# Attention in steps of two groups: the order of the matmuls, the maxima and the copies on each engine

## The chip, the core and the metric

The kernel is one program on one core of a Trainium2 chip. The metric is the time of one execution on the device, in microseconds (us). The core has five engines that each work through their own list of instructions in order and meet only through semaphores: TensorE (PE; its weight loads are shown apart as PEld), VectorE (DVE), ScalarE (ACT), GpSimd (POOL) and SyncE (SP), which here only issues DMAs. Matmul results land in PSUM, which has eight banks; each result tile here takes one bank.

## The reference: what is computed

Attention over 4 batches, 12 heads, 448 positions and head size 64, in which the heads are mixed before and after the softmax, and behind it two feed-forward parts without a softmax (1792 tokens, 768 wide):

```python
scores = scale * np.matmul(q, k.transpose(0, 1, 3, 2))
scores = np.einsum('bhij,hg->bgij', scores, w_pre)
scores = scores - np.max(scores, axis=-1, keepdims=True)
attn = np.exp(scores)
attn = attn / (np.sum(attn, axis=-1, keepdims=True) + 1e-09)
attn = np.einsum('bhij,hg->bgij', attn, w_post)
x = np.matmul(attn, v)          # then, after a transpose to (tokens, 768):
h = (x @ w1) * (x @ w2) @ w3 @ w_out
g = np.maximum(0.01 * (h @ w_in), h @ w_in)
out = g @ w_out2
```

## The kernel before

The queries of a batch are dealt into chunks of 120, 120, 120 and 88. A chunk is cut into **blocks** of ten queries and pairs of blocks form a **group** of twenty queries; there are 180 blocks in 92 groups (six groups a chunk, five in the short one, whose last group has one block). These kinds of work make up the attention:

- `qk`: the scores of a pair of heads for a whole chunk, two chunks ahead (tile `pq`, L221, two banks `qa`); ScalarE copies them out (`evict`, L229), and they are stored to DRAM (`sdr`).
- `relayout` (L262): a group's scores come back from DRAM with queries times heads on the partitions (tile `sr`), four groups ahead.
- `premix` (L273): the first mixing of heads as a matmul with `kpre`; a block's result fills one bank `pm`.
- `softmax`: VectorE takes the maximum of each row (`mx`, L280), ScalarE the exponential with its sum (`e`, `sm`, L283). `weigh`: GpSimd adds 1e-9 to the sum (L290), VectorE takes the reciprocal `rc` (L292), GpSimd multiplies it into the mixing weights (`kr`, L294).
- `postmix` (L308): the second mixing, four matmuls a block in the program (the trace has two records for each matmul of this kind), result in a bank `po`; VectorE or ScalarE copies it to `ap` (L315).
- `av` (L328): the product with `v` for two heads; two of them share a bank `px`, which VectorE copies to `y` (L337). It needs the whole chunk's `ap`.
- `conversions` (the generator `filler`): the weights for the later parts are turned from 64-bit words to 32-bit on ScalarE and VectorE (tile `wc`, L98 to L109) in small steps between the other work; `q_split` and `k_split` split inputs in two parts (VectorE L80, L185).

The attention is under a manual schedule, so each engine's instructions stand in the order of the code. The main loop takes one group a step: the maxima and exponentials of group k, then the `postmix` of group k-2 block by block between the `weigh` calls of group k, then one `qk`, in every other step two `av`, and `premix` of group k+1. Copies out of `po` go to VectorE, but for the second block of every other step. `px` has a bank of its own.

At the end the loop runs out of `qk`, and the first weights of the next part, `fold` (L542), are prepared: `wo` in eight pieces (L553, L554) and `ws` from `wc`. `marks` and `ends` hold instructions of the loop behind which these are placed.

Of the kernel before, what the change touches and what calls it, by code (L numbers as in the profile page):

```python
# [23 lines left out]
def attention_moe_kernel(ctx: ExitStack, tc, qt, kt, vt, w_pre, w_post, w1, w2, w3t, w_out, w_in2, w_out2, out):  # L24
# [7 lines left out]
    nc = tc.nc  # L32
# [11 lines left out]
    AHEAD, QAHEAD, START, LAG = 4, 2, 7, 2  # L44
# [26 lines left out]
    banks = {"qa": 2, "pm": 3, "po": 2, "px": 1}  # L71
# [50 lines left out]
    def attention():  # L122
        with ExitStack() as es:
# [50 lines left out]
            srt, pms, ets, sms, krs, apt = {}, {}, {}, {}, {}, {}  # L174
# [101 lines left out]

            def softmax(n):
                pm = pms.pop(n)
                mx = wk.tile([P, 1], F32, tag="mx", name="mx")
                nc.vector.tensor_reduce(out=mx, in_=pm, axis=AX.X, op=ALU.max, negate=True)  # L280
                e = wk.tile([P, S], F32, tag="e", name="e", bufs=6)
                sm = wk.tile([P, 1], F32, tag="sm", name="sm")
# [5 lines left out]
            def weigh(n):  # L288
                sm = sms.pop(n)
                nc.gpsimd.tensor_scalar(out=sm, in0=sm, scalar1=1e-9, scalar2=None, op0=ALU.add)  # L290
                rc = wk.tile([P, 1], F32, tag="rc", name="rc")
# [7 lines left out]
            def postmix(n, copy):  # L299
# [15 lines left out]
                copy(ap[:, :, :, o:o + nb], po)  # L315

            def av(b, c, p):
# [5 lines left out]
                if r == 0:  # L323
                    pxs[0] = bank("qa" if g and (b, c) == order[-1] else "px", [P, 2, CH], "px")
# [115 lines left out]
            q_split(0, 2)()  # L440
            premix(0)
            todo, since = [], 0
            for k in range(NG + LAG):
# [3 lines left out]
                evict()  # L447
                if k < NG:
                    b, c, t, nt = where[k]
                    ci = order.index((b, c))  # L450
                    for n in groups[k]:
                        softmax(n)
                done = k - LAG
                for i in range(2):
                    if done >= 0 and i < len(groups[done]):
                        on_act = i and (t % 2 or k >= NG - 8)
                        postmix(groups[done][i], nc.scalar.copy if on_act else nc.vector.tensor_copy)
                    if k < NG and i < len(groups[k]):
                        weigh(groups[k][i])
                if k < NG:  # L460
                    if k + AHEAD < NG:
                        relayout(k + AHEAD)
                    ps = []
                    if ci + QAHEAD < len(order):
                        ps = [t] if nt == NPAIR else [4, 5] if t == 4 else [t]
                        if ci == 0:
                            ps = ([], [0], [1], [2], [3], [4, 5])[t]
                    if ps:
                        qk(*order[ci + QAHEAD], ps[0])
                since += 1  # L470
                if ci + QAHEAD < len(order):
                    n = 2 * (since % 2)
                else:
                    n = 1 if k < NG and len(todo) <= nt - since + 1 else 2
                for _ in range(min(n, len(todo))):
                    av(*todo.pop(0))
                if done >= 0 and done < NG - 1 and where[done][2] == where[done][3] - 1:
                    todo += [(*where[done][:2], p) for p in range(NPAIR)]
                    since = 0
                if k < NG:  # L480
                    for p in ps[1:]:
                        qk(*order[ci + QAHEAD], p)
                    if k + 1 < NG:
                        premix(k + 1)
# [10 lines left out]
                if k < NG:  # L495
                    if c == 0 and t == 2:
                        v_prep(b)
# [266 lines left out]
```

## Time and profile before

| | |
|---|---|
| median of 3 runs | 1332.93 us (1329.87 to 1333.66) |
| the profiled execution | 1328.94 us, of which its span of instructions is 1327.2 us |
| TensorE busy | 1309.5 us, 99% of the span |
| VectorE, ScalarE, GpSimd busy | 882.1, 599.7 and 168.1 us |
| mean granted TensorE clock | 0.992 of full speed |
| DMA | 220.01 MB, mean 166 GB/s |

A view of the timeline has one line for instructions of one kind that follow each other: start, time from the first start to the last end, engine, line of the kernel, operation, tiles written and read, shape, number, and in brackets how long the engine had been idle and what ended that. Matmuls overlap in the array: one that takes 0.27 us can start 0.10 us behind the one before, so the pace is read from starts, not from durations.

### The profile page before, as it was taken

Reading aid. Unit: us, or ns where it says so; the run is one execution under the profiler, and the core shown is the slowest. Engines: PE = TensorE matmul, PEld = TensorE weight load, DVE = VectorE, ACT = ScalarE, POOL = GpSimd, SP = SyncE. Lnnn points to the kernel's source line nnn. Section 1 sums busy time; section 2 is a strip of 40 time slices with the busy share of each in tenths; the row PEclk is TensorE's granted clock in tenths of the full one; section 3 lists DMA queues with packets and bytes.
Section 4 is the critical chain, followed back from the end, with each engine's and each line's share of the span. In section 5 each row is a group of like instructions: output and inputs, shape, how many; then the busy total and the mean of one; then the engine's idle time right before and its main releaser. Section 6 shows DMA issues by size and latency. Waiting matters only on the chain.

```text
span 1327.2 us, 23071 instructions
## 1 busy us (share of the span) xinstructions
PE 1309.5 (99%) x8926; PEld 1126.1 (85%) x8926; DVE 882.1 (66%) x1536; ACT 599.7 (45%) x1161; POOL 168.1 (13%) x371
## 2 busy tenths in 40 slices
PE   8999999999999899999999999999999999999998
PEld 5677777777777899898989999999898989999998
DVE  5577777776657676673469678695773449596762
ACT  5566666666556343332245525162433226444240
POOL 1343444444344000000000000000000000000000
PEclk8899999999999999999999999999999999999999
DMA  7988999998987763421424333256331324342302
GB/s 242 308 282 252 287 308 279 314 298 269 270 225 206 249 200 123 119 80 57 126 72 146 117 119 97 94 149 209 99 108 48 103 95 124 115 143 90 125 1 84
DMA packets 137825, 220.01 MB, mean 166 GB/s; under 512 B 20148, under 2 KB 119220, under 8 KB 137140
## 3 DMA queue, kind: packets, MB, share of 16 engines
q1 hardware_dynamic: 137716, 218.54, 53.0%
q8 instruction: 71, 1.16, 0.4%
q14 instruction: 38, 0.31, 0.1%
HBM read 161.62 MB, written 56.89 MB: 165 GB/s over the span
## 4 chain that ended last, share of the span: by engine, by line
PE 94%; DMA 3%; DVE 1%; issue 0%; SPq 0%; ACT 0%; POOL 0%; ACTq 0%; POOLq 0%; DVEq 0%
PE pm L630 44%; PE po L699 18%; PE po L308 11%; PE pm L273 6%; PE px L328 5%; PE pq L221 5%; PE pw L565 5%; DMA sr<-sdr 1%; DMA ws<-w3s 1%; DMA ql<-in_q_dram 1%; PE turn L254 1%; DMA sdr<-s 0%; SPq L262 0%; ACT e L283 0%; DVE wc L106 0%
## 5 line engine op out<-in xcount | busy, mean ns | idle before, releaser
L630 PE MATMUL pm<-x,ws 128*128 128x512 f32 (+1 forms) x2304 | 466.8, 363 | 0.0
L630 PEld LDWEIGHTS pm<-x,ws 128*128 128x128 f32 x2304 | 417.6, 188 | 47.7
L699 PE MATMUL po<-ws,g 128*128 128x384 f32 x1344 | 234.2, 334 | 0.0
L699 PEld LDWEIGHTS po<-ws,g 128*128 128x128 f32 x1344 | 233.1, 188 | 0.0
L308 PEld LDWEIGHTS po<-kr,e 128*112 128x112 f32 x1440 | 155.9, 179 | 67.3 <-POOL kr L294 26.1
L308 PE MATMUL po<-kr,e 128*112 128x120 f32 (+1 forms) x1440 | 173.4, 274 | 1.8 <-DVE ap L315 1.8
L283 ACT ACTIVATE e<-pm,mx 128x448 f32<-128x448 f32 x180 | 112.7, 631 | 131.7 <-DVE mx L280 130.7
L80 DVE TENSOR_TENSOR ws<-wc,ws 128x768 fp32r<-128x768 f32 (+1 forms) x103 | 100.1, 974 | 83.7 <-ACT ws L77 83.4
L98 ACT ACTIVATE wc<-wr 128x768 f32<-128x768 f32 (+3 forms) x122 | 104.9, 863 | 80.7 <-DVE ws L80 62.7
L77 ACT ACTIVATE ws<-wc 128x768 fp32r<-128x768 f32 (+1 forms) x103 | 87.9, 857 | 106.8 <-PE po L699 74.0
L294 POOL TENSOR_SCALAR kr<-kpost,rc 128x120 f32<-128x120 f32 x180 | 125.0, 694 | 67.5 <-DVE rc L292 59.2
L280 DVE TENSOR_REDUCE mx<-pm 128x1 f32<-128x448 f32 x180 | 104.1, 617 | 22.9 <-PE pm L273 17.9
L630 PE MATMUL pm<-h,ws 128*128 128x512 f32 (+1 forms) x576 | 116.3, 363 | 0.0
L630 PEld LDWEIGHTS pm<-h,ws 128*128 128x128 f32 x576 | 104.3, 188 | 11.7
L109 DVE SCALAR_TENSOR_TENSOR wc<-wr,wc 128x768 uint32<-128x768 uint32 (+3 forms) x122 | 110.7, 908 | 1.5
L106 DVE SCALAR_TENSOR_TENSOR wc<-wr,wc 128x768 uint32<-128x768 uint32 (+3 forms) x122 | 110.2, 906 | 1.1
L273 PE MATMUL pm<-sr,kpre 60*64 60x448 f32 x720 | 96.3, 575 | 5.0 <-DMA sr<-sdr 4.9
L229 ACT ACTIVATE s<-pq 120x448 f32<-120x448 f32 (+1 forms) x180 | 88.5, 543 | 20.9 <-PE pq L221 19.8
L100 DVE TENSOR_SCALAR wc<-wc 128x768 f32<-128x768 f32 (+3 forms) x122 | 65.1, 534 | 46.2 <-ACT wc L98 46.0
L315 DVE COPY ap<-po 112x480 f32<-112x480 f32 (+1 forms) x135 | 86.8, 643 | 1.7 <-PE po L308 1.5
L328 PEld LDWEIGHTS px<-ap,vs 112*64 112x64 f32 x1536 | 75.2, 138 | 14.8 <-issue 13.2
L221 PE MATMUL pq<-ks,qs 64*120 64x448 f32 (+1 forms) x576 | 85.2, 402 | 2.2 <-ACT qs L77 1.3
(56 smaller groups left out, 980.0 us busy)
## 6 DMA issues: line engine op xcount, KB each, us to landing
sr<-sdr SPq DMA_DIRECT2D x176, 210.0 KB
sdr<-s SPq DMA_DIRECT2D x36, 840.0 KB
wr<-in_moe_w_dram SPq DMA_DIRECT2D x32, 768.0 KB
wr<-in_moe_w_in_dram SPq DMA_DIRECT2D x32, 768.0 KB
wr<-in_moe_w_out_dram SPq DMA_DIRECT2D x32, 768.0 KB
sdr<-s SPq DMA_DIRECT2D x12, 616.0 KB
wr<-in_moe_w_dram SPq DMA_DIRECT2D x7, 1024.0 KB
wr<-in_moe_w_out_dram SPq DMA_DIRECT2D x16, 384.0 KB
```

The source lines that it names most:

```text
L98: nc.scalar.activation(out=cf, in_=hi.bitcast(F32), func=ACTF.Abs)
L106: lambda: nc.vector.scalar_tensor_tensor(out=c, in0=hi, scalar=0xC0000000, in1=c, op0=ALU.bitwise_and, op1=ALU.bitwise_or),
L109: lambda: nc.vector.scalar_tensor_tensor(out=c, in0=lo, scalar=29, in1=c, op0=ALU.logical_shift_right, op1=ALU.bitwise_or),
L221: nc.tensor.matmul(pq[e][:m], qst[b, c][rows, p, x, :m], kst[b, p][rows, y, :], start=(j == 0), stop=(j == 2))
L273: nc.tensor.matmul(pms[n][g * Q:(g + 1) * Q], kpre[rows], sr[rows, g, :], start=True, stop=True)
L280: nc.vector.tensor_reduce(out=mx, in_=pm, axis=AX.X, op=ALU.max, negate=True)
L283: ends["act"] = nc.scalar.activation(out=e, in_=pm, func=ACTF.Exp, bias=mx, scale=1.0, accum_out=sm)
L294: ends["pool"] = nc.gpsimd.tensor_scalar(out=kr, in0=kpost, scalar1=rc, scalar2=None, op0=ALU.mult)
L308: nc.tensor.matmul(po[:, jc].rearrange("p h (g i) -> p h g i", g=2), e[:, jc * JP:(jc + 1) * JP], kr, start=True, stop=True,)
L328: nc.tensor.matmul(px[e * D:(e + 1) * D, r, :ni], vst[b][:, jc, 2 * p + e, :], ap[:, jc, 2 * p + e, :ni], start=(jc == 0), stop=(jc == NJ ...
L630: nc.tensor.matmul(dst, wt[:, a, kk, :], x[:, kk, c, c0:c0 + w], start=(kk == 0 and j == 0), stop=(kk == kn - 1 and j == 2),)
L699: nc.tensor.matmul(po, g[:, m, a, t * P:(t + 1) * P], wts[m][:, c, 0, cs], start=(m == 0 and j == 0), stop=(m == FQ - 1 and j == 2),)
```

## The change

The loop takes two groups, four blocks, a step. `premix` of both groups stands together at a step's end, `postmix` of the four blocks of the step before stands together, and one to three `qk` stand around them. `top` takes the four maxima, first in the step on VectorE; the exponentials stay in `softmax`. Of four copies out of `po` VectorE has the first and the third, ScalarE the second and the fourth. `px` loses its bank to `pm` (now four) and takes turns with the four blocks in the two banks `po`. What was done once a group at a step's end is moved into `side`; the conversions start with group 10, not 7, their first loads with group 5, not 2, and the loads of `v` and `k` are one group later. The pieces of `wo` are tied to other marks, and `ends` now also holds the copies.

The diff, cut (`pairs` returns the `qk` of a group as before):

```diff
-    AHEAD, QAHEAD, START, LAG = 4, 2, 7, 2
+    AHEAD, QAHEAD, START = 4, 2, 10
...
-    banks = {"qa": 2, "pm": 3, "po": 2, "px": 1}
+    banks = {"qa": 2, "pm": 4, "po": 2}
...
-                t = bank("px", [P, P], "turn")
+                t = bank("po", [P, P], "turn")
...
+            def top(n):
+                mxs[n] = wk.tile([P, 1], F32, tag="mx", name="mx", bufs=8)
+                nc.vector.tensor_reduce(out=mxs[n], in_=pms[n], axis=AX.X, op=ALU.max, negate=True)
+
             def softmax(n):
-                pm = pms.pop(n)
-                mx = wk.tile([P, 1], F32, tag="mx", name="mx")
-                nc.vector.tensor_reduce(out=mx, in_=pm, axis=AX.X, op=ALU.max, negate=True)
+                pm, mx = pms.pop(n), mxs.pop(n)
...
+                sm = wk.tile([P, 1], F32, tag="sm", name="sm", bufs=8)
...
-                copy(ap[:, :, :, o:o + nb], po)
+                ends["act" if copy == nc.scalar.copy else "dve"] = copy(ap[:, :, :, o:o + nb], po)
...
-                    pxs[0] = bank("qa" if g and (b, c) == order[-1] else "px", [P, 2, CH], "px")
+                    pxs[0] = bank("qa" if g and (b, c) == order[-1] else "po", [P, 2, CH], "px")
...
+            def side(k):
+
...
+                while lows:
+                    lows.pop(0)()
+                if c == 0 and t == (2 if b else 3):
+                    v_prep(b)
+                if (t == 4 or k == 0) and ci + QAHEAD + (1 if k == 0 else 2) < len(order):
+                    q_load(*order[ci + QAHEAD + (1 if k == 0 else 2)])
+                if b + 1 < B and c == NC - 3 and t in (2, 4, 5):
+                    k_load(b + 1, (2, 4, 5).index(t))
+                if k >= START or k == START - 5:
+                    for _ in range(2 if k >= START and t in (2, 5) else 1):
+                        next(filler, None)
+
...
             premix(0)
-            todo, since = [], 0
-            for k in range(NG + LAG):
+            premix(1)
+            todo = []
+            for k in range(0, NG + 2, 2):
+                evict()
                 flush()
                 while later:
                     stores.append(later.pop(0))
-                evict()
-                if k < NG:
-                    b, c, t, nt = where[k]
-                    ci = order.index((b, c))
-                    for n in groups[k]:
-                        softmax(n)
-                done = k - LAG
-                for i in range(2):
-                    if done >= 0 and i < len(groups[done]):
-                        on_act = i and (t % 2 or k >= NG - 8)
-                        postmix(groups[done][i], nc.scalar.copy if on_act else nc.vector.tensor_copy)
-                    if k < NG and i < len(groups[k]):
-                        weigh(groups[k][i])
-                if k < NG:
-                    if k + AHEAD < NG:
-                        relayout(k + AHEAD)
-                    ps = []
...
-                    if ps:
-                        qk(*order[ci + QAHEAD], ps[0])
-                since += 1
-                if ci + QAHEAD < len(order):
-                    n = 2 * (since % 2)
-                else:
-                    n = 1 if k < NG and len(todo) <= nt - since + 1 else 2
-                for _ in range(min(n, len(todo))):
+                now = [g for g in (k, k + 1) if g < NG]
+                done = [g for g in (k - 2, k - 1) if g >= 0]
+                ps = [x for g in now for x in pairs(g)]
+                fresh = [n for g in now for n in groups[g]]
+                old = [n for g in done for n in groups[g]]
+                if ps:
+                    qk(*ps.pop(0))
+                for g in now:
+                    if g + AHEAD < NG:
+                        relayout(g + AHEAD)
+                for n in fresh:
+                    top(n)
+                for i in (0, 2):
+                    if i == 0:
+                        for n in fresh[:2]:
+                            softmax(n)
+                        evict()
+                    elif not now:
+                        while todo:
+                            av(*todo.pop(0))
+                    for j in (i, i + 1):
+                        if j < len(old):
+                            postmix(old[j], nc.scalar.copy if j % 2 else nc.vector.tensor_copy)
+                    if i == 0:
+                        for n in fresh[2:]:
+                            softmax(n)
+                    for n in fresh[i:i + 2]:
+                        weigh(n)
+                if len(ps) > 1:
+                    qk(*ps.pop(0))
+                for g in done:
+                    b, c, t, nt = where[g]
+                    if t == nt - 1 and (b, c) != order[-1]:
+                        todo += [(b, c, p) for p in range(NPAIR)]
+                for _ in range(min(4 if len(todo) > NPAIR else 2, len(todo))):
                     av(*todo.pop(0))
-                if done >= 0 and done < NG - 1 and where[done][2] == where[done][3] - 1:
-                    todo += [(*where[done][:2], p) for p in range(NPAIR)]
-                    since = 0
-                if k < NG:
-                    for p in ps[1:]:
-                        qk(*order[ci + QAHEAD], p)
-                    if k + 1 < NG:
-                        premix(k + 1)
-                    if ci + QAHEAD + 1 < len(order) and t == (4 if ci == 0 or c == NC - 2 else 3):
-                        lows.append(q_split(*order[ci + QAHEAD + 1]))
-                    if b + 1 < B:
-                        if c == NC - 3 and t >= 4:
-                            lows.append(k_split(b + 1, t - 4))
-                        if c == NC - 2 and t < 4:
-                            lows.append(k_split(b + 1, t + 2))
+                for x in ps:
+                    qk(*x)
+                for g in (k + 2, k + 3):
+                    if g < NG:
+                        premix(g)
+                for g in now:
+                    side(g)
                 while lows:
                     lows.pop(0)()
                 marks.append(dict(ends))
...
-            tags = itertools.cycle(("pm", "qa", "po", "pm", "px", "qa", "po", "pm"))
+            tags = itertools.cycle(("pm", "qa", "pm", "po", "pm", "qa", "pm", "po"))
...
                 for kk in range(KF):
-                    with behind(ends if kk >= KF - 2 else marks[kk - LAG - KF]):
+                    with behind(marks[min(kk // 2 - 4, -1)]):
                         hi_act(wo[:, kk, 0], wo[:, kk, 1].bitcast(F32))
                         lo_dve(wo[:, kk, 1], wo[:, kk, 1].bitcast(F32), wo[:, kk, 0])
```

TensorE in the middle of the attention (`pm` is `premix`, `po` `postmix`, `px` `av`, `pq` `qk`), first before, two steps and the start of a third:

```order
L273 MATMUL pm<-sr,kpre 64x448 x4
L308 MATMUL po<-kr,e 112x120 x8
L221 MATMUL pq<-ks,qs 120x448 x6
L328 MATMUL px<-ap,vs 64x88 x16
L273 MATMUL pm<-sr,kpre 64x448 x4
L308 MATMUL po<-kr,e 112x120 x8
L221 MATMUL pq<-ks,qs 120x448 x6
```

Each group's `pm` and `po` form stretches of their own there. Of the change, one step of two groups:

```order
L273 MATMUL pm<-sr,kpre 64x448 x8
L221 MATMUL pq<-ks,qs 120x448 x6
L310 MATMUL po<-kr,e 112x120 x16
L330 MATMUL px<-ap,vs 64x120 x16
L221 MATMUL pq<-ks,qs 120x448 x6
```

The same matmuls stand in five stretches in place of seven. Over the attention the listings have 46 stretches of `pm` (91 before), 47 of `po` (92) and 45 of `px` (50).

VectorE in the middle of the attention, before, two steps (`mx` the maxima, `ap` a copy out of `po`, `rc` the reciprocals, `y` the copy out of `px`, `wc` conversions, `ks` a split):

```order
L280 TENSOR_REDUCE mx<-pm 128x1 x2
L315 COPY ap<-po 112x48x10
L292 RECIPROCAL rc<-sm 128x1
L315 COPY ap<-po 112x48x10
L292 RECIPROCAL rc<-sm 128x1
L337 COPY y<-px 128x240
L185 TENSOR_TENSOR ks<-kl,ks 128x448
L100 TENSOR_SCALAR wc<-wc 128x384
L280 TENSOR_REDUCE mx<-pm 128x1 x2
L315 COPY ap<-po 112x48x10
L292 RECIPROCAL rc<-sm 128x1 x2
```

A copy stands directly behind two maxima there. Of the change, one step and the first row of the next:

```order
L279 TENSOR_REDUCE mx<-pm 128x1 x4
L317 COPY ap<-po 112x48x10
L294 RECIPROCAL rc<-sm 128x1 x2
L317 COPY ap<-po 112x48x10
L294 RECIPROCAL rc<-sm 128x1 x2
L339 COPY y<-px 128x240
L106 SCALAR_TENSOR_TENSOR wc<-wr,wc 128x384
L109 SCALAR_TENSOR_TENSOR wc<-wr,wc 128x384
L279 TENSOR_REDUCE mx<-pm 128x1 x4
```

The first copy moved behind four maxima, the second of VectorE's copies behind two reciprocals.

VectorE at the end of the attention, from the last maximum on, before (`wo` and `wc` are weights of the next part):

```order
L280 TENSOR_REDUCE mx<-pm 128x1
L315 COPY ap<-po 112x48x10
L292 RECIPROCAL rc<-sm 128x1
L80 TENSOR_TENSOR wo<-wo 128x768
L337 COPY y<-px 128x240
L80 TENSOR_TENSOR wo<-wo 128x768
L315 COPY ap<-po 112x48x10
L100 TENSOR_SCALAR wc<-wc 128x1024 x2
L103 TENSOR_SCALAR wc<-wc 128x1024 x2
L106 SCALAR_TENSOR_TENSOR wc<-wr,wc 128x1024 x2
L337 COPY y<-px 128x240
L109 SCALAR_TENSOR_TENSOR wc<-wr,wc 128x1024
```

The last copies stand there among the pieces of `wo` and behind steps on `wc`. Of the change:

```order
L317 COPY ap<-po 112x48x10
L317 COPY ap<-po 112x48x8
L339 COPY y<-px 128x240
L80 TENSOR_TENSOR wo<-wo 128x768 x2
L100 TENSOR_SCALAR wc<-wc 128x1024 x2
L103 TENSOR_SCALAR wc<-wc 128x1024 x2
L106 SCALAR_TENSOR_TENSOR wc<-wr,wc 128x1024 x2
L109 SCALAR_TENSOR_TENSOR wc<-wr,wc 128x1024 x2
L80 TENSOR_TENSOR ws<-wc,ws 128x1024 x2
```

All copies of the attention now stand ahead of the last two `wo` and of the eight steps on `wc`.

## Rows read from the trace of the kernel before

**Rows 1.** The page, busy time and share of the span of each engine.

```profile
PE 1309.5 (99%) x8926; PEld 1126.1 (85%) x8926; DVE 882.1 (66%) x1536; ACT 599.7 (45%) x1161; POOL 168.1 (13%) x371
```

**Rows 2.** Windows: length, busy PE PEld DVE ACT POOL, granted clock, DMA share, GB/s.

```profile
200.00:300.00 100.00, 100.00 (x1059) 71.54 (x1061) 73.88 (x175) 64.83 (x166) 41.83 (x89) 1.00 0.94 300
300.00:411.00 111.00, 111.00 (x1189) 79.53 (x1181) 72.22 (x170) 66.09 (x169) 45.40 (x104) 1.00 0.89 254
411.00:447.00 36.00, 30.28 (x326) 24.82 (x327) 27.17 (x45) 17.67 (x33) 7.46 (x16) 0.95 0.68 209
```

**Rows 3.** Timeline of TensorE, some of the stretches of 203 to 222 us.

```profile
206.35 0.87 PE L221 MATMUL pq<-ks,qs 64*120 64x448 f32 x6
207.16 0.98 PE L273 MATMUL pm<-sr,kpre 60*64 60x448 f32 x8
...
212.49 0.98 PE L273 MATMUL pm<-sr,kpre 60*64 60x448 f32 x8
```

**Rows 4.** The same view in windows of a fraction of a microsecond.

```profile
203.62 0.61 PE L273 MATMUL pm<-sr,kpre 60*64 60x448 f32 x4
...
204.04 0.56 PE L273 MATMUL pm<-sr,kpre 60*64 60x448 f32 x4
204.53 0.36 PE L308 MATMUL po<-kr,e 128*112 128x120 f32 x1
...
204.72 0.57 PE L308 MATMUL po<-kr,e 128*112 128x120 f32 x4
...
205.13 0.57 PE L308 MATMUL po<-kr,e 128*112 128x120 f32 x4
```

**Rows 5.** Chain that ended last, 370 to 400 us: start, time, what.

```profile
378.00 1.79 PE px L328 x32
...
386.04 0.97 PE px L328 x16
```

**Rows 6.** Timeline of one group on four engines, 379 to 384 us.

```profile
379.72 0.98 PE L273 MATMUL pm<-sr,kpre 60*64 60x448 f32 x8
...
380.81 1.16 DVE L280 TENSOR_REDUCE mx<-pm 128x1 f32<-128x448 f32 x2 [0.56 <-PE pm L273]
...
381.88 0.65 DVE L315 COPY ap<-po 112x480 f32<-112x480 f32 x1
...
382.34 0.22 POOL L290 TENSOR_SCALAR sm<-sm 128x1 f32<-128x1 f32 x1 [2.87 <-ACT e L283]
...
382.60 0.16 DVE L292 RECIPROCAL rc<-sm 128x1 f32<-128x1 f32 x1
...
382.93 0.59 POOL L294 TENSOR_SCALAR kr<-kpost,rc 128x120 f32<-128x120 f32 x1 [0.36 <-DVE rc L292]
...
383.60 0.22 POOL L290 TENSOR_SCALAR sm<-sm 128x1 f32<-128x1 f32 x1
383.85 0.16 DVE L292 RECIPROCAL rc<-sm 128x1 f32<-128x1 f32 x1 [1.09 <-POOL sm L290]
```

**Rows 7.** Timeline where TensorE and a copy wait for each other.

```profile
427.97 0.65 DVE L315 COPY ap<-po 112x480 f32<-112x480 f32 x1
...
428.76 1.04 PE L308 MATMUL po<-kr,e 128*112 128x120 f32 x8 [1.77 <-DVE ap L315]
...
429.85 0.57 ACT L315 COPY ap<-po 112x480 f32<-112x480 f32 x1 [0.84 <-PE po L308]
```

**Rows 8.** Groups of VectorE, 66.9 to 411 us: busy us, mean ns, idle before.

```profile
L185 DVE TENSOR_TENSOR ks<-kl,ks 128x448 fp32r<-128x448 f32 x18 | 11.1, 616 | 0.0
...
L109 DVE SCALAR_TENSOR_TENSOR wc<-wr,wc 128x384 uint32<-128x384 uint32 (+1 forms) x19 | 10.6, 556 | 0.3
```

**Rows 9.** Timeline of TensorE near the start of the attention.

```profile
54.66 2.42 PE L273 MATMUL pm<-sr,kpre 60*64 60x448 f32 x8 [2.33 <-DMA sr<-sdr]
```

**Rows 10.** Windows behind it, columns as in rows 2.

```profile
57.08:62.00 4.92, 4.92 (x27) 4.02 (x30) 1.60 (x5) 2.70 (x7) 1.62 (x4) 0.58 0.99 331
```

**Rows 11.** Groups of VectorE at the end of the attention, 426 to 437 us.

```profile
L106 DVE SCALAR_TENSOR_TENSOR wc<-wr,wc 128x1024 uint32<-128x1024 uint32 x2 | 2.4, 1216 | 0.0
```

More of the change, by code (lines that the diff above doesn't have):

```diff
@@ L173, in attention @@
             kst, vst, qst, st = {}, {}, {}, {}
-            srt, pms, ets, sms, krs, apt = {}, {}, {}, {}, {}, {}
+            srt, pms, mxs, ets, sms, krs, apt = {}, {}, {}, {}, {}, {}, {}
             def k_load(b, g):
@@ L290, in weigh @@
                 nc.gpsimd.tensor_scalar(out=sm, in0=sm, scalar1=1e-9, scalar2=None, op0=ALU.add)
-                rc = wk.tile([P, 1], F32, tag="rc", name="rc")
+                rc = wk.tile([P, 1], F32, tag="rc", name="rc", bufs=8)
                 ends["dve"] = nc.vector.reciprocal(out=rc, in_=sm)
@@ L440, in attention, with pairs @@
             q_split(0, 2)()
+            def side(k):
+                b, c, t, nt = where[k]
+                ci = order.index((b, c))
+                if ci + QAHEAD + 1 < len(order) and t == (4 if ci == 0 or c == NC - 2 else 3):
+                    lows.append(q_split(*order[ci + QAHEAD + 1]))
+                if b + 1 < B:
+                    if c == NC - 3 and t >= 4:
+                        lows.append(k_split(b + 1, t - 4))
+                    if c == NC - 2 and t < 4:
+                        lows.append(k_split(b + 1, t + 2))
+                while lows:
[9 more added lines that the diff above has]
+                        next(filler, None)
+            def pairs(k):
+                b, c, t, nt = where[k]
+                ci = order.index((b, c))
+                if ci + QAHEAD >= len(order):
+                    return []
+                ps = [t] if nt == NPAIR else [4, 5] if t == 4 else [t]
+                if ci == 0:
+                    ps = ([], [0], [1], [2], [3], [4, 5])[t]
+                return [(*order[ci + QAHEAD], p) for p in ps]
             premix(0)
-            todo, since = [], 0
-            for k in range(NG + LAG):
+            premix(1)
+            todo = []
+            for k in range(0, NG + 2, 2):
+                evict()
                 flush()
@@ L494, in attention @@
                 marks.append(dict(ends))
-                if k < NG:
-                    if c == 0 and t == 2:
-                        v_prep(b)
-                    if (t == 4 or k == 0) and ci + QAHEAD + (1 if k == 0 else 2) < len(order):
-                        q_load(*order[ci + QAHEAD + (1 if k == 0 else 2)])
-                    if b + 1 < B and c == NC - 3 and t in (0, 1, 3):
-                        k_load(b + 1, (0, 1, 3).index(t))
-                    if k >= START or k == START - 5:
-                        for _ in range(2 if k >= START and t in (2, 5) else 1):
-                            next(filler, None)
             for _ in filler:
```

5 lines of the change are left out of this document (removed).

## The prediction

> **What bounds the kernel now.** I read the page first: TensorE is busy 99% of the span, no other engine over 66% [rows 1]. Then the windows of the attention: from 200 to 411 us TensorE is busy all the time at a granted clock of 1.00, VectorE 74% and 65%, ScalarE less, the DMA share .94 and .89; only the end, 411 to 447 us, has idle time, 5.7 us [rows 2]. So in the middle no wait is left to take away: time can come only out of TensorE's own work, and a new wait there costs its full length. Behind 447 us the change only permutes bank tags, and I cost that at nothing. One pair of groups takes 8.87 us (212.49 less 203.62) [rows 3, 4].
>
> **What the change saves.** The matmuls stay, but they stand in fewer stretches, and a stretch loses something at its ends. For `po` the matmuls run at .1025 us each (sets of four start at 204.72 and 205.13), so 16 should take 1.64; from 204.53 to 206.35 they take 1.82. Joining two stretches saves .18 [rows 3, 4]. For `px` 32 take 1.79 and 16 take .97, so joining saves .15 [rows 5]. A `pm` stretch takes .91, .42 for its first round and .49 for its last [rows 3, 4]; a middle round isn't shown alone, so I take .17, between the other two. A step of two groups therefore saves .35, and .50 where it joins `px` too, as at the end of the attention, where no `qk` is left.
>
> By the order 45 junctions of `pm`, 45 of `po` and 5 of `px` go: 7.7 + 8.1 + .7 = 16.5 us, 1.2%, if nothing new waits.
>
> **What the change adds: banks.** Five users now share two banks in each step: the four blocks, then `px`. Block 3 needs the bank of copy 1, `px` that of copy 3. I work a step out from durations of before; time 0 is its first `pm` matmul. `pm` 2 x .91 - .17 and `pq` .81 (206.35 to 207.16) put the first `po` matmul at S = 2.46 [rows 3, 4].
>
> Block one is ready for its copy 1.09 behind S (428.76 to 429.85); a copy on VectorE takes .65, and TensorE goes on .14 behind its end (427.97 + .65 to 428.76) [rows 7]. So the bank is back 1.88 behind S, where TensorE wants it after 2 x .91 - .09 = 1.73: it stops .15. ScalarE's copy takes .57 [rows 7], and block four comes in time.
>
> Copy three can't start before two reciprocals, which stand ahead of it in VectorE's list. The second waits for GpSimd, which handles one block after the other. By one group's timeline: copy start to reciprocal .72 (381.88 to 382.60), to `kr` .33, to the next `sm` .67, to its reciprocal .25, then about half of that one's .16 [rows 6]: copy three starts 2.05 behind copy one, and `px` 2.05 + .65 + .14 = 2.84 behind it, at S + 3.93. Unhindered it would start at S + 3.46 (two joined stretches). Each step with `qk` loses .47 and gains .35: +.12. If the reciprocals were not in the way, copy three would be ready at S + 1.88 + 1.09, `px` at S + 3.76, and the loss is .30: a net gain of .05. Both ends stay for the range.
>
> At the end there is no `pq`, S is 1.65, and the four maxima decide: the first comes 1.09 behind the first `pm` matmul (379.72 to 380.81), two take 1.07 to the copy [rows 6], so copy one starts at 3.23, not 2.74, and `px` at 6.07 against 5.11. Loss .96, gain .50: +.46.
>
> There are some 35 steps of the first kind from 62 us on and 5 of the second: 35 x .12 = +4.2 and 5 x .46 = +2.3.
>
> **Chunk ends.** In seven steps `px` reads the copy that ScalarE makes of block four. That block starts at S + 2.75, so its copy ends at S + 2.75 + 1.09 + .57 = S + 4.41 and `px` starts about .53 later than above: 7 x .53 = +3.7 (none if the first `px` of a chunk can go a step later; it can't by the order).
>
> **VectorE's other work.** Conversions and splits now stand in a block behind `y` instead of once a group. Between `y` (about 8.5) and the point from which late maxima hold up copy one (9.0 + 1.09 + .3 of slack) some 1.8 us fit. A split of `ks` takes .62 and a conversion .56 [rows 8]; 13 steps hold more than 1.8 us, together 6.5 us too much by these durations. What hides the rest is that stretch; if it is gone, each conversion costs its .56. Since a step that already stops gives VectorE a little more time, I take 5, ends 0 and 6.5. Two of VectorE's steps on `wo` now fall into steps of the end, ahead of the maxima: 768 columns each, at 3/4 of the 1.22 that 1024 take [rows 11], +1.8.
>
> **Moved loads and exponentials.** Weights to convert are loaded three groups later, `v` and `k` one. Before, TensorE stood 2.33 us for a group's scores at 54.66, and the next `pm` took 2.42 [rows 9] where .98 is usual [rows 3]: 3.8 us in all, the clock .58 up to 62 us [rows 10]. Scores that stand behind fewer loads in SyncE's list may come sooner: I take -3.5. If all of the slow stretch goes, -8; if later loads collide in the same way, +3. Four `pm` banks come free with the fourth exponential, which is through some 2 us before the next `pm`; at nothing.
>
> **The end.** The last copies now stand ahead of conversions; the wait of 1.77 for a copy [rows 7] should go. But the eight steps on `wc` (up to 1.22 each [rows 11]) start only behind the last copy, and the next part needs their result. I take -1.5, ends -3 and +4.
>
> **Sum.** +4.2 + 2.3 + 3.7 + 5 + 1.8 - 3.5 - 1.5 = +12.0 us. On the profiled execution's 1328.9 that is 1341, on the median, which is 4 higher, 1345; I say **1343**. About 4 us, 0.3%, is what a measurement of this kernel can tell from none. Low end of the costs: 35 x -.05, the end steps even, half the chunk ends, no overflow, -8 and -3: about -9. High end: overflow 6.5, +3 and +4: about +25.
>
> **Rivals.**
>
> *Copies don't hold TensorE (faster).* Place: the third `po` block and `px` of each step. The point from which it decides is a stop of .35 a step. For it: VectorE is busy 74% [rows 2], so no throughput is lacking; my sum is of latencies, each seen once or twice, and an earlier copy by .2 turns the sign. Then 40 steps save 35 x .35 + 5 x .5 = 14.8, and with -3.5 and -1.5 at both ends and some chunk ends, about -16 in all: 1313 on the profiled execution's time, 1317 on the median. With half of the stops (21 us in all by the working above) it is -5.5, so 1323 to 1327. Against it: the chain po, copy, po of 1.88 lies in every step, and the window is 1.73. A limit on it: DMA's .94 [rows 2] becomes .98 if a pair takes 8.52, so it can't go much further. Chance .22.
>
> *Nothing to measure.* Stops of .30 a step, the overflow covered, chunk ends as worked out: -1.8 + 2.3 + 3.7 + 1.8 - 3.5 - 1.5 = +1, so 1330 to 1334. For it: the gain and the cost of a step are nearly equal, whichever way the reciprocals fall. Chance .18.
>
> *The clock.* TensorE would now stop twice in each 9 us, where rows 2 show 211 us without a stop at 1.00. Before, a stop of 2.33 us was followed by a matmul stretch at half clock [rows 9] and .58 for 5 us more [rows 10], which costs some 3.5 us; if one step in ten did so, four of them add 14 to the sum, 1357; one in four, 1375. Against it: the stops are .15 to .5 us. In 411 to 447 us, with 5.7 us of stops, the clock is still .95 [rows 2]. Chance .05. The Trainium skill ("TensorE: Matmul & The Clock Gate", section "A second HAM failure mode: psum-queue depth-cycling") tells of a kernel that cycles through PSUM banks, idles briefly between groups of matmuls, and whose clock goes up and down with it. By that rule this change makes just such a kernel, and 1357 to 1375 would be its result. The trace of before has no stops as short and regular, so it neither confirms nor denies it.
>
> **Numbers.** Forecast (slower, 1337 to 1358) .55, the clock .05, no change .18, faster .22. So faster .22, same .18, slower .60. The range is 1316 to 1358: it takes in most of the faster case and leaves out its best end and the clock.
>
> **What would show it.** In the changed profile TensorE's waits would name `ap` on VectorE, some 40 of about .15 ahead of a third block and as many of .3 ahead of `px`; a `pm` of two groups takes 1.65, four blocks of `po` 3.5, and a step about 9.0 instead of 8.87. At chunk ends `px` waits for ScalarE's `ap`. VectorE's maxima come late behind two or more conversions. The stop at 54.66 is shorter or gone. The forecast is wrong if steps take 8.6 or less, if the stops are there but stand where VectorE waits for something else, or if the granted clock falls below 1.00 in the middle.

## The result, and the profile after

The changed kernel takes 1339.45 us, the median of 6 runs (1336.62 to 1342.19), beside 1332.17 us before (6 runs): a ratio of 1.0058, 95% interval 1.0041 to 1.0075. It is slower by 0.6%, 3.6 us under the forecast of 1343. The profiled execution took 1338.76 us with a span of 1336.8, 9.6 more than before.

The page's first row and two windows, with the columns of [rows 1, 2]:

```profile
PE 1304.2 (98%) x8926; PEld 1129.8 (85%) x8926; DVE 855.3 (64%) x1493; ACT 623.0 (47%) x1204; POOL 155.7 (12%) x371
```

```profile
200.00:300.00 100.00, 96.78 (x1043) 71.32 (x1043) 64.31 (x160) 69.02 (x171) 36.13 (x86) 1.00 0.94 292
300.00:411.00 111.00, 107.66 (x1152) 79.47 (x1150) 63.53 (x160) 71.13 (x181) 42.26 (x102) 1.00 0.91 262
```

TensorE is busy 5.3 us less, but the span is longer: in the middle, where it never stood, it now stands 3% of the time, at a granted clock that stays 1.00. The list of TensorE's waits over the whole run (engine, line, what it waited for: us in total, times, longest) names them:

```profile
PE po L310 <- DVE rc L294: 8.5, 18, 1.4
PE pw L591 <- ACT ws L77: 5.2, 1, 5.2
PE px L330 <- ACT ap L317: 3.9, 6, 0.7
PE pm L273 <- DMA sr<-sdr: 3.9, 2, 3.6
PE pq L221 <- ACT s L229: 2.1, 3, 1.1
```

The first line names a reciprocal, since that ends just ahead of the matmul; what the third `po` block waits for by the order is the bank of the copy in front of that reciprocal, and it starts .15 behind that copy's end, as a `po` block did before (.14 [rows 7]). One ordinary step, the timeline of TensorE and VectorE:

```profile
377.78 1.74 PE L273 MATMUL pm<-sr,kpre 60*64 60x448 f32 x16
...
379.44 0.84 PE L221 MATMUL pq<-ks,qs 64*88 64x448 f32 x6
...
380.21 3.78 PE L310 MATMUL po<-kr,e 128*112 128x120 f32 x32
...
381.32 0.66 DVE L317 COPY ap<-po 112x480 f32<-112x480 f32 x1 [0.24 <-PE po L310]
381.90 0.15 DVE L294 RECIPROCAL rc<-sm 128x1 f32<-128x1 f32 x1
...
383.14 0.17 DVE L294 RECIPROCAL rc<-sm 128x1 f32<-128x1 f32 x1 [1.09 <-POOL sm L292]
...
383.23 0.65 DVE L317 COPY ap<-po 112x480 f32<-112x480 f32 x1
...
383.92 1.86 PE L330 MATMUL px<-ap,vs 112*64 112x120 f32 x32
```

The step is 8.71 us long (386.49 less 377.78; 8.77 where `pq` has 120 rows). Before, the same work took 8.82 (the row below to 379.72 [rows 6]; 8.87 where `pq` has 120 rows), so an ordinary step is .10 shorter. Timeline of before:

```profile
370.90 0.98 PE L273 MATMUL pm<-sr,kpre 60*64 60x448 f32 x8
```

`pm` takes 1.66 (to 379.44), as worked out, `po` 3.71 (380.21 to 383.92), .25 more than 3.46. The .25 lies ahead of the third block, in three narrow windows:

```profile
381.84 0.61 PE L310 MATMUL po<-kr,e 128*112 128x120 f32 x2
```

```profile
382.13 0.53 PE L310 MATMUL po<-kr,e 128*112 128x120 f32 x3
```

```profile
382.29 0.37 PE L310 MATMUL po<-kr,e 128*112 128x120 f32 x2
```

The last matmul of the second block starts at 381.84, the next at 382.13, .29 later instead of .10, and the one behind it .16 later, again instead of .10. `px` starts .04 behind the end of copy three and .20 behind the start of the last `po` matmul; it lies the same .20 behind in run 5 at 147.65 us, where copy three had ended .6 us earlier, so nothing is lost there.

A step that is not ordinary, in the view of the chain that ended last (start, time, what):

```profile
286.41 0.04 DVE y L339
...
286.73 0.67 DVE ks L185
287.40 0.47 DVE wc L109
287.87 0.53 DVE ks L185
288.41 0.28 DVE wc L100
...
288.71 0.36 DVE wc L103
289.07 2.13 DVE mx L279 x4
291.20 0.56 DVE ap L317
...
291.91 1.88 PE po L310 x16
```

With gaps of at most .3 us the chain leads from `y` through two splits and three conversions and the four maxima to the first copy and the third `po` block. `po` takes 4.90 us in this step, 1.19 more than in an ordinary one: .46 are this stop and .73 the wait of `px` at a chunk's end, which is shown below. The list of waits has 13 stops of the third block between 62 and 394 us, 4.7 us in all; ahead of each of them VectorE's list runs from `y` through splits or conversions and the maxima to the copy, and in one alone (at 189.20 us, 1.04 us) it waits for ScalarE's half of a split.

Two more kinds, from timelines of ScalarE and TensorE:

```profile
188.59 0.58 ACT L77 ACTIVATE ks<-kl 128x448 fp32r<-128x448 f32 x1 [2.80 <-DMA kl<-in_k_dram]
189.07 0.96 ACT L229 ACTIVATE s<-pq 120x448 f32<-120x448 f32 x2
...
189.65 1.30 PE L221 MATMUL pq<-ks,qs 64*120 64x448 f32 x6 [1.13 <-ACT s L229]
```

```profile
266.21 0.57 ACT L317 COPY ap<-po 112x480 f32<-112x480 f32 x1
...
266.82 0.63 PE L330 MATMUL px<-ap,vs 112*64 112x120 f32 x8 [0.65 <-ACT ap L317]
```

In the first ScalarE stands for a load of `k`, the copy of the scores stands behind that split, and `pq` waits for the copy. The second is a chunk's end as forecast, six times. And the end, where the first `pw` is the next part's:

```profile
439.66 0.56 DVE L317 COPY ap<-po 112x384 f32<-112x384 f32 x1 [3.41 <-PE po L310]
...
442.18 1.29 DVE L100 TENSOR_SCALAR wc<-wc 128x1024 f32<-128x1024 f32 x2
...
449.28 6.91 PE L591 MATMUL pw<-wo,ws 128*128 128x384 f32 x22 [5.15 <-ACT ws L77]
```

To set the traces side by side I counted the matmul records that each had started, weighted by their pace. At 60.65 us the changed kernel is 2.9 us ahead of before, at 394.4 us 6.6 behind, at 425.8 us 7.5 behind, at the first `pw` 8.7 behind (449.28 and 440.57), and at the end 9.6.

### The profile page after: what moved, and what is told of

It is laid out like the page before. It is cut to its first block, busy times and chain, and to the rows that moved or that the text cites. A ratio compares the mean times of both kernels' runs of the same rounds, so it can differ in the third digit from the quotient of the medians.

```text
span 1336.8 us, 22982 instructions
## 1 busy us (share of the span) xinstructions
PE 1304.2 (98%) x8926; PEld 1129.8 (85%) x8926; DVE 855.3 (64%) x1493; ACT 623.0 (47%) x1204; POOL 155.7 (12%) x371
## 4 chain that ended last, share of the span: by engine, by line
PE 86%; DVE 6%; DMA 3%; POOL 2%; issue 2%; ACT 1%; SPq 0%; POOLq 0%; DVEq 0%; ACTq 0%
PE pm L656 43%; PE po L725 17%; PE po L310 7%; PE pw L591 5%; PE pm L273 4%; PE px L330 4%; PE pq L221 4%; DVE mx L279 2%; DMA sr<-sdr 2%; POOL kr L296 1%; DMA kl<-in_k_dram 1%; DVE ap L317 1%; DVE ks L185 1%; PE turn L254 1%; DMA sdr<-s 1%
## 5 line engine op out<-in xcount | busy, mean ns | idle before, releaser
L310 PE MATMUL po<-kr,e 128*112 128x120 f32 (+1 forms) x1440 | 170.7, 272 | 10.0 <-DVE rc L294 8.5
L296 POOL TENSOR_SCALAR kr<-kpost,rc 128x120 f32<-128x120 f32 x180 | 112.5, 625 | 118.2 <-DVE rc L294 77.4
L279 DVE TENSOR_REDUCE mx<-pm 128x1 f32<-128x448 f32 x180 | 100.2, 616 | 16.7 <-PE pm L273 13.6
L294 DVE RECIPROCAL rc<-sm 128x1 f32<-128x1 f32 x180 | 29.0, 161 | 121.7 <-POOL sm L292 121.7
L273 PE MATMUL pm<-sr,kpre 60*64 60x448 f32 (+1 forms) x720 | 86.7, 567 | 4.0 <-DMA sr<-sdr 3.9
L330 PE MATMUL px<-ap,vs 112*64 112x120 f32 (+1 forms) x1536 | 83.5, 262 | 4.6 <-ACT ap L317 3.9
```

Source lines behind the costliest of these rows:

```text
L273: nc.tensor.matmul(pms[n][g * Q:(g + 1) * Q], kpre[rows], sr[rows, g, :], start=True, stop=True)
L279: nc.vector.tensor_reduce(out=mxs[n], in_=pms[n], axis=AX.X, op=ALU.max, negate=True)
L296: ends["pool"] = nc.gpsimd.tensor_scalar(out=kr, in0=kpost, scalar1=rc, scalar2=None, op0=ALU.mult)
L310: nc.tensor.matmul(po[:, jc].rearrange("p h (g i) -> p h g i", g=2), e[:, jc * JP:(jc + 1) * JP], kr, start=True, stop=True,)
L330: nc.tensor.matmul(px[e * D:(e + 1) * D, r, :ni], vst[b][:, jc, 2 * p + e, :], ap[:, jc, 2 * p + e, :ni], start=(jc == 0), stop=(jc == NJ ...
```

## The experiments

Theory A: TensorE loses more in the shared banks and behind VectorE's late maxima, ScalarE's late copies and the chunk ends than the joined stretches give. Rival B, in a form of its own for each run: removing a stop only hands the lateness on. All ratios are to the kernel before, timed beside each run; so a difference between two runs is better taken from their ratios than from their medians.

**1. The last `qk` ahead of `av`.** The two loops change places:

```diff
+                for x in ps:
+                    qk(*x)
                 for _ in range(min(4 if len(todo) > NPAIR else 2, len(todo))):
                     av(*todo.pop(0))
-                for x in ps:
-                    qk(*x)
```

> Only the order of the last qk and the av of a step is swapped on TensorE, so that .8 us of qk lie between the fourth po block and px. In the changed kernel px stands .65 us for ScalarE's copy at five chunk ends, .73 with the stretch end, 3.7 us in all, and pq stands 1.1, .36 and .15 us for ScalarE's copy of the scores ahead of it. Theory A (px waits for the last copy of its chunk): the five stops are gone, and the three pq stops become shorter because the copies of the scores get 1.8 us more: 5 to 6 us less, ratio to before about 1.002. Rival B (the lateness is handed on, another wait takes it): the px stops go but the time stays within 1 us of the changed kernel, ratio about 1.005 to 1.006.

Measured: 1353.70 us, ratio 1.0152 (1.0122 to 1.0181), 14 us more than the changed kernel by the medians, 12.5 by the ratios. Between 62 and 404 us:

```profile
PE po L310 <- DVE rc L294: 16.6, 20, 1.4
```

The stops of `px` are gone, as both said, but the third block stands 16.6 us instead of 4.7: `px` ends .8 us later in the step, so `y` and everything behind it on VectorE, the maxima among it, come later too. The stops of `pq` did not become shorter either (4.6 us in six). A was wrong in sign and B in size; VectorE's list behind `y` is a bound of its own.

**2. The copies of the scores ahead of the conversions on ScalarE.**

```diff
+                evict()
                 for g in now:
                     side(g)
```

> At the end of a step the copies of the scores out of pq stand ahead of the conversions on ScalarE instead of behind them. Theory A (a conversion on ScalarE that waits for its data or for VectorE holds the copies of the scores, and these hold the next pq): the stops of pq at 189.65, 317.29 and 336.21 and the slow pm and pq stretches beside them go, 3.2 us less; ratio to before 1.003. Rival B: they are caused by loads or by VectorE, and stay or are replaced by later exponentials; within 1 us of the changed kernel.

Measured: 1379.25 us, ratio 1.0342 (1.0318 to 1.0366), 40 us more by the medians, 38 by the ratios. ScalarE and VectorE in one step:

```profile
202.63 0.98 ACT L229 ACTIVATE s<-pq 120x448 f32<-120x448 f32 x2 [2.54 <-PE pq L221]
203.50 0.58 ACT L77 ACTIVATE ks<-kl 128x448 fp32r<-128x448 f32 x1
...
204.11 0.63 DVE L185 TENSOR_TENSOR ks<-kl,ks 128x448 fp32r<-128x448 f32 x1 [1.85 <-ACT ks L77]
...
206.52 2.21 DVE L279 TENSOR_REDUCE mx<-pm 128x1 f32<-128x448 f32 x4
...
209.44 2.26 PE L310 MATMUL po<-kr,e 128*112 128x120 f32 x16 [2.16 <-DVE rc L294]
```

`pq` no longer waits for ScalarE's copies. But ScalarE now waits 2.54 us for `pq` before it makes its half of the split, VectorE waits 1.85 us for that half with the maxima behind it, and the third block stops 2.16 us; there are 22 such stops between 62 and 404 us, 33.9 us in all. So the two halves of a split and the four maxima form one chain.

**3. The first group's conversions behind copy three.**

```diff
+                    if i and now:
+                        side(now[0])
                     for n in fresh[i:i + 2]:
                         weigh(n)
...
-                for g in now:
+                for g in now[1:]:
                     side(g)
```

> The splits and conversions of the first group of a step are put between VectorE's copy of the third block and the last two reciprocals, instead of behind y with those of the second group. Theory A (VectorE reaches the four maxima late behind a block of conversions, and the first copy and the third po block late behind them): the stops of the third block above .13 us, 4.7 us in all over 14 steps, fall to under 1.5 us; some 3 to 4 us less, ratio to before about 1.003. Rival B: the conversions only move the lateness to the reciprocals and from there to kr and the po block of the next step: no gain, within 1 us of the changed kernel, or slower.

Measured: 1343.30 us, ratio 1.0073 (1.0050 to 1.0096): B. The chain ahead of a late third block:

```profile
198.15 0.57 ACT ks L77
...
198.75 0.63 DVE ks L185
199.38 0.27 DVE wc L103
199.65 0.08 DVE rc L294
...
202.97 2.13 DVE mx L279 x4
```

VectorE waits 1.23 us for ScalarE's half there, and two reciprocals, `y` and the maxima follow late. The third block's stops grow from 4.7 to 13.4 us between 62 and 394 us. So fewer conversions ahead of the maxima are not enough: where they stand now they make VectorE wait, and the lateness comes back to the maxima.

**4. The copies taken out of `ends`.**

```diff
-                ends["act" if copy == nc.scalar.copy else "dve"] = copy(ap[:, :, :, o:o + nb], po)
+                copy(ap[:, :, :, o:o + nb], po)
```

> The copies out of po are taken out of the instructions that the first conversions of the next part stand behind; nothing else. Theory A (the eight conversion steps that now start behind the last copy hold the first matmul of the next part for 5.15 us, against 1.35 before): that stop falls to about 1.5 to 3 us, while copies at the end come later behind conversions, up to 2 us back: 1 to 3 us less, ratio to before about 1.004. Rival B (the stop is set by something else, the load of w3s or wo): the stop stays at 5 us and the time within .5 us of the changed kernel.

Measured: 1341.80 us, ratio 1.0063 (1.0043 to 1.0083), no gain: the stop fell as A said, the time did not. TensorE's wait of 5.15 for ScalarE's `ws` fell to 1.4, with 1.3 and .6 for other parts of the weights, but in the window from 432 us

```profile
432.00:444.00 12.00, 8.59 (x102) 7.67 (x102) 11.46 (x18) 5.06 (x7) 2.42 (x3) 0.86 0.01 2
```

TensorE now stops among the last copies, at a clock of .86, and VectorE is busy 11.46 of 12 us. In the changed kernel it is busy 9.25 of the 9.30 us from 440.0 to 449.3. So VectorE is the bound of the end on either side of the copies, and the first `pw` starts at 448.75 instead of 449.28.

**5. Two maxima behind the first reciprocal.** With what the first three showed, the place to put work is where VectorE waits for GpSimd, 1.09 us ahead of the second reciprocal.

```diff
-                for n in fresh:
+                for n in fresh[:2]:
                     top(n)
...
                     if i == 0:
+                        for n in fresh[:1]:
+                            weigh(n)
+                        for n in fresh[2:]:
+                            top(n)
                         for n in fresh[2:]:
                             softmax(n)
-                    for n in fresh[i:i + 2]:
+                    for n in fresh[max(i, 1):i + 2]:
                         weigh(n)
```

> Two of the four maxima go back behind the first copy and the first reciprocal, into the 1.1 us in which VectorE waits for GpSimd ahead of the second reciprocal. Theory A (what varies from step to step is that VectorE comes late to the four maxima, and the first copy out of po with it): the first copy starts 1.07 us sooner where it waited behind maxima. The stops of the third po block fall from 8.5 us to about 2 (the .13 a step at a time that the shared bank costs stays, and is below what the list of waits shows), the steps at the end from 7.60 to about 7.2 us: 6 to 7 us less than the changed kernel, ratio to before about 1.000 to 1.001. Rival B (lateness is handed on: later exponentials and sums hold the second reciprocal and the third copy): the stop moves from the third block to px, time within 1.5 us of the changed kernel, ratio 1.005 or more.

Measured: 1336.26 us, ratio 1.0017 (1.0006 to 1.0028), 3.2 us less than the changed kernel by the medians and 5.5 by the ratios: the way of A, a little less. Between 62 and 394 us no third block waits for VectorE's reciprocal any more, and the steps at the end take 7.17 us instead of 7.60. VectorE there:

```profile
397.72 0.66 DVE L317 COPY ap<-po 112x480 f32<-112x480 f32 x1 [0.54 <-PE po L310]
398.30 0.15 DVE L294 RECIPROCAL rc<-sm 128x1 f32<-128x1 f32 x1
398.37 1.14 DVE L279 TENSOR_REDUCE mx<-pm 128x1 f32<-128x448 f32 x2
399.55 0.16 DVE L294 RECIPROCAL rc<-sm 128x1 f32<-128x1 f32 x1
```

The second reciprocal comes 1.25 us behind the first, as without the maxima: they cost nothing in this place.

**6. The conversions dealt between the reciprocals.** `side` only counts them; `give()` does one:

```diff
+                    if i:
+                        give()
                     for n in fresh[i:i + 2]:
                         weigh(n)
+                        if n == fresh[i]:
+                            give()
```

> The conversion steps leave the end of a step and are dealt one by one into the next step, between the reciprocals, where VectorE waits for GpSimd; the four maxima stay first. Splits of q and k stay. Theory A: the block ahead of the maxima is at most two splits (1.25 us), inside the 1.8 us that fit; the third block's stops fall to about 3 us (the end of the attention keeps its own), and on ScalarE the conversions no longer stand ahead of the copies of the scores, so the stops of pq and the slow pm beside them (5 us) shrink to about 2: 6 us less, ratio about 1.001. Rival B (the conversions wait for ScalarE there and hold the reciprocals, copy three or the last copy of a chunk): px stops longer, no gain or a loss as in the run with a group's conversions behind copy three, ratio 1.006 or more.

Measured: 1337.34 us, ratio 1.0023 (1.0004 to 1.0042): the way of A, 4.7 us less than the changed kernel by the ratios where 6 were expected. Between 62 and 394 us the third block's stops for the reciprocal fall from 4.7 to .9 us; those of `pq` for ScalarE stay.

**7. Both.**

> Both of these together; conversions stand behind copy three and between the last two reciprocals. Theory A: the gains overlap on the third block (there is only one set of stops) and add on pq: 8 to 10 us less than the changed kernel, ratio to before about .998 (2 to 3 us faster than before). Rival B: no better than the better one of the two, ratio 1.003 or more.

Measured: 1333.17 us, ratio .9993 (.9977 to 1.0008): 8.7 us less than the changed kernel by the ratios, where the two alone make 10.2. The gains nearly add, and the time is that of before.

**8. Both, and `qk` ahead of `av`.**

> The same, and the last qk of a step stands ahead of av on TensorE. That cost 14 us alone, because y and everything behind it on VectorE came .8 us later. Theory A (VectorE has slack now): the stops of px at five chunk ends go (3.7 us) and the third block's stay small, 3 us less than without the swap, ratio to before about .996. Rival B (the order of qk and av costs by itself, or there is no slack): slower than without the swap by 3 us or more.

Measured: 1329.83 us, ratio .9971 (.9954 to .9988): A. The swap that cost 12 to 14 us alone now gives some 3, though the two intervals just overlap. TensorE's waits between 62 and 387 us are

```profile
PE pq L221 <- ACT s L229: 3.5, 4, 1.5
PE po L310 <- ACT ap L317: 0.2, 1, 0.2
```

and this version is faster than both kernels, by 0.3% in the case of the kernel before. The stop of .25 ahead of the third block, too short for this list, stands in its steps as well (their `po` takes 3.71). No run takes that away, so what a third bank for `po` would give is open.

**9. The kernel before with the later loads alone.** `START` 10 and the loads of `v` and `k` as changed.

> The kernel before with one part of the change alone: conversions from group 10 and their loads from group 5 on, v and k loads one group later. In the changed kernel TensorE is 2.9 us further at 61 us than before, the only large gain beside the 3.5 us of the joined stretches. Theory A (that gain is the later loads: the scores of the first groups stand behind fewer of them): the stop of 2.33 us at 54.66 and the half clock behind it go here too, 2 to 4 us less, ratio to before .9975 to .9985. Rival B (it is the order of the matmuls at the start, two groups of scores at once and qk ahead): the stop for scores stays and the time stays within 1 us, ratio .999 to 1.001.

Measured: 1332.97 us, ratio .9999 (.9982 to 1.0016). The stop for scores at 54.66 is gone, as A said, but the sum is B's: loads of `k` that are late now make ScalarE wait, and `pq` behind it.

```profile
74.41 0.58 ACT L77 ACTIVATE ks<-kl 128x448 fp32r<-128x448 f32 x1 [4.23 <-DMA kl<-in_k_dram]
...
75.91 1.27 PE L221 MATMUL pq<-ks,qs 64*88 64x448 f32 x6 [1.31 <-ACT s L229]
```

So the later loads give at the start and take back behind it: by the count of matmul records this run is 3.9 us ahead of before at 61 us, level at 200 us and 1.1 behind at 394 us.

**10. Run 8 with the loads of `k` at their old places**, `t in (0, 1, 3)`.

> The kernel with two maxima in the gap, conversions between reciprocals and qk ahead of av, and the loads of k one or two groups earlier again, as in the kernel before. Theory A (ScalarE stands for a load of k at 184.92 there, its copy of the scores comes late behind it and pq stops 1.47 us, and the steps from 173 to 220 us are 1.0 us longer in sum): these stops go, 3 to 4 us less than with the late loads, ratio to before about .9945. Rival B (the DMA queues are full there, the earlier loads of k make the scores late instead): no gain, stops of pm for scores, ratio .997 or more.

Measured: 1329.60 us, ratio .9976 (.9958 to .9994). The stop of 1.47 us is gone, but the time is the same within the intervals. Where it went isn't settled: other waits in the trace differ by less than a microsecond each.

**11. The same with the copies out of `ends`.**

> The same with the copies taken out of the instructions that the next part's first conversions stand behind. In the changed kernel alone this took the stop of the next part from 5.15 to 1.4 us, but the last px and po stretches became longer by as much. Theory A (VectorE's chain of conversions is the bound of the end, whichever side of the copies it stands): within 1.5 us of the run with early loads of k. Rival B (the earlier steps left VectorE late there, now it has time): 2 to 4 us less.

Measured: 1331.18 us, ratio .9988 (.9973 to 1.0003), beside .9976: 1.6 us more, the same within the intervals, and not the 2 to 4 us less of B. It fits A, by which VectorE's chain bounds the end.

**12. Run 8 with the two groups' `premix` apart.**

```diff
                 if ps:
                     qk(*ps.pop(0))
+                if k + 1 < NG and k:
+                    premix(k + 1)
...
-                for g in (k + 2, k + 3):
-                    if g < NG:
-                        premix(g)
+                if k + 2 < NG:
+                    premix(k + 2)
```

> The kernel with two maxima in the gap, conversions between the reciprocals and qk ahead of av, but the two groups' premix apart again, with the first qk of the step between them: one junction of pm less in each step that has a qk, and nothing else. Theory A (a stretch of pm loses at its ends what the profile shows, .16 a junction): a step takes 8.87 to 8.93 us in place of 8.71 to 8.77 where nothing else waits, some 36 steps, 5 to 6 us more, ratio to before about 1.0015. Rival B (the modelled ends make the stretch look longer, or the wait for the shared bank hides it): no change, ratio .996 to .998.

Measured: 1337.49 us, ratio 1.0034 (1.0022 to 1.0047), .63% above run 8.

```profile
61.14 0.98 PE L273 MATMUL pm<-sr,kpre 60*64 60x448 f32 x8
...
70.00 0.98 PE L273 MATMUL pm<-sr,kpre 60*64 60x448 f32 x8
```

A step takes 8.86 us there, .15 more: some 36 such steps are 5.4 us, A's 5 to 6. Of the rest of the 8.4 one stop of `pq` for ScalarE of 2.1 us and what follows it is a part; all of it isn't accounted for. So the gain of a junction is real; the places where something waits are what ate it.

## Why the prediction was right, and where its sum was off

The direction came as forecast, and so did VectorE's block ahead of the maxima, the chunk ends and the clock at 1.00. The wait in the shared banks was forecast to cost an ordinary step more than the joined stretches give, and it costs less; two terms had the wrong sign, and one kind of stop was not in the sum. That the sum came near was therefore luck in part. The range, 1316 to 1358, held faster and slower, so of its claims on the time only the direction was put to the test.

- **The ordinary step** was the step of the sum that failed, in sign too: +.12 us was forecast, -.10 measured (8.77 against 8.87, and 8.71 against 8.82 where `pq` has 88 rows), so 35 of them give -3.5 instead of +4.2. The saving was right (`pm` 1.66; run 12 measures .15 for that junction). The stop ahead of block three was forecast .15 and is .25. But `px` was to lose .32 more behind copy three, and it loses nothing: the copy starts 1.91 behind copy one (381.32 to 383.23), not 2.05, since the first reciprocal follows the copy's start by .58 (381.90), not by the .72 of [rows 6], where GpSimd's sum had only just ended (382.34 + .22); `px` follows its end after .04, not .14 [rows 7]; and the later start of the third block has moved the moment at which `px` would be wanted to just that point. The .14 of [rows 7] is the price of a `po` block: the third block pays it here too (381.32 + .66 to 382.13 is .15), but `px` starts .04 behind the copy also where it clearly waits (266.21 + .57 to 266.82).
- **Chunk ends**: +3.7 forecast for seven of .53, six stops of .65, 3.9 in all, measured. Right.
- **VectorE's block ahead of the maxima**: +5 forecast, 4.7 measured from 62 to 394 us. Right; and runs 5 and 6, which take either the maxima or the conversions out of that chain, get the time back. That the block can also hang on ScalarE's halves of the splits, as in runs 2 and 3, I had not seen; in the changed kernel it does so in one step.
- **Not in the sum**: `pq` behind ScalarE's copies, which stand behind conversions and splits (2.1 us in the list, and again some .4 each time until the second bank is free), and scores that came late once. The four steps with such stops take 10.17, 10.54, 10.38 and 10.19 us, some 5 us too much. With these the middle comes to what the records show: from 2.9 ahead to 6.6 behind is 9.5 us; -3.5, +3.3 (five of the chunk ends lie there), +4.7 and some 5 give 9.5.
- **The start**: -3.5 forecast, -2.9 measured. Run 9 shows that the later loads alone give such a gain, and that they take it back by 200 us, in part by late loads of `k`, which no term had.
- **The steps at the end**: +2.3 and +1.8 forecast, +.9 measured. A step takes 7.60 instead of 7.42, +.19 and not +.46, again since `px` loses nothing behind copy three; the step with `wo` takes 8.59, one more microsecond, not two. And before lost 1.2 us in one slow pair there (at 412.75 us `pm` took 2.00 and `po` 1.98, where .91 and 1.82 are usual), which the changed kernel does not have.
- **The end**: -1.5 forecast, +1.2 up to the first `pw` measured and .9 more behind it. The sign was wrong, inside the ends given (-3 and +4): the eight steps on `wc` cost more than the copies had waited. Run 4, which lets them start sooner again, brings the first `pw` only .5 forward, so the order of copies and steps is not all of it.

With the measured terms the sum is near the 9.6 us that the spans differ by; the +12.0 was right in sign and 2.4 too large because errors of both signs, the largest 7.7 us, cancelled. That the clock would fall did not come true: with stops of .2 to 1.4 us in most steps the windows show 1.00. So the rule of the Trainium skill's "A second HAM failure mode: psum-queue depth-cycling" ("TensorE: Matmul & The Clock Gate"), a clock that goes up and down with brief idle times, did not show itself here; the time that its rule would have given, 1357 to 1375, is not the measured one.

## What to carry to other kernels

Fewer, longer stretches of matmuls are worth something (.15 us for a junction of `pm` here), but a step that does twice as much makes every other engine's work come in larger blocks; follow each block to the first instruction behind it that TensorE waits for. In a list in order, long work belongs into the places where the engine waits anyway: two maxima and the conversions cost little or nothing between the reciprocals, while in one block they held the third block 4.7 us in all. The same edit, `qk` ahead of `av`, cost 12 to 14 us where VectorE had no slack and gave 3 where it had: undo the bound first, then judge the edit.

## What was not expected of the hardware

A `px` matmul that waited for a copy starts .04 us behind its end (266.21 + .57 to 266.82), a `po` block .15 behind (381.32 + .66 to 382.13), as in the trace of before (.14 [rows 7]); why the two differ no run shows. And once a `po` stretch has stopped, its second start comes after .16 us, not at the pace of .10, so a stop of .19 (.29 less .10) costs .25.
